# A new instruction order, new SBUF addresses and new PSUM banks for a hand-scheduled two-branch kernel

## The chip, the cores and the metric

The kernel runs on one core of a Trainium2 chip. The metric is device time in microseconds, as the median of the runs of one program. Five instruction streams work side by side and meet only through semaphores: PE (TensorE; its weight loads are listed apart as PEld), DVE (VectorE), ACT (ScalarE), POOL (GpSimd) and SP (SyncE, which here only issues DMAs). Each takes its own instructions strictly in the order in which they were written.

## What is computed

Two independent branches share one launch, and their outputs are concatenated. Branch A is a linear attention with softmax feature maps. Branch B is a state-space convolution: a kernel `K` of 2048 taps per channel is built from 256 complex modes, and the signal is convolved with it.

```python
def _A_ref(x, wqkv, w_phi, wo):            # x [1,2048,448], 16 heads of 28
    q, k, v = ...                           # x @ wqkv
    pq = einsum("bhsd,hdf->bhsf", q, w_phi); pk = ...
    phi_q = concat([softmax(pq), softmax(-pq)]); phi_k = ...
    kv = einsum("bhsf,bhsd->bhfd", phi_k, v); z = einsum("bhsf->bhf", phi_k)
    num = einsum("bhqf,bhfd->bhqd", phi_q, kv)
    den = einsum("bhqf,bhf->bhq", phi_q, z) + 1e-6
    return (num / den) @ wo
def _B_ref(u, A, B, C, log_dt, Dskip):     # u [1,2048,448], 256 modes
    P = exp(dt * A * l)                     # l = 0..2047
    K = einsum("dn,dnl,dn->dl", C, P, dt * B).real
    y = irfft(rfft(pad(u)) * rfft(pad(K)))[:2048]
    return y + u * Dskip
out = concat([a, b], axis=-1)
```

## The kernel before

Every step of the kernel is first recorded as a unit of a `Plan` (1399 units): what it costs on which engines, what it reads and writes, and a function that emits it. Nothing is scheduled while the kernel is built. Three tables of numbers at the top of the file decide everything that the program's text leaves open:

- `ORDER` lists all 1399 units in the order in which they are emitted, each with the letter of its engine: P for PE, D for DVE, A for ACT, G for POOL, S for SP. It sets the order within each engine's stream, and the engine itself where a unit may run on more than one.
- `HOMES` gives the byte address in SBUF of every buffer. Two buffers that share bytes make the later writer wait for the earlier reader.
- `BANKS` gives the PSUM bank of every accumulator. A matmul into a bank waits until the former tile there has been read.

```python
for x, bank in zip(self.tiles, BANKS):
    x.make(int(bank))
for token in ORDER.split():
    u = self.units[int(token[:-1])]
    u["fn"](names[token[-1]])
```

The units that the rest of the text speaks of, with the helper line under which the profile lists them:

- `mms` (L359): a group of matmuls into one PSUM tile. All PE work is listed there.
- `copy` (L350): a PSUM tile into SBUF, on ACT or on DVE as the order says. `act` (L340) is an activation on ACT; Exp and Sin need a table load between them (ACT_TABLE_LOAD). `tt` (L330) is elementwise work on DVE.
- `total` (L389 on DVE, L391 on POOL): an addition in SBUF, either by DVE or by a DMA from POOL's queue that adds.
- `dma` (L374): a transfer issued by SP, ACT or POOL. `turn` (L380): a transposing DMA, always from SP.

Branch B works in eight column groups `k`. For each, `dampings`, `rotations` and `hi_tables` make factors, `damp` combines them on DVE, and `build_k` multiplies them on PE: two units of 112 matmuls each, one into rows of 32 partitions and 49 columns, so that a unit has 224 instructions and is short. Two column groups make one channel group `gi` (0 to 3). Its taps go through `scatter_k`: four DMAs into a buffer `Kb`, then thirteen DMAs that place rows of `Kb` in `Kt` (the K rows), and one that fills `KX`. `kernel_spectrum` multiplies `Kt` with a transform table (units ks), `conv_group` multiplies the spectra on DVE (units conv), and `inverse` transforms back on PE, copies to `OB` and stores by SP. The spectrum of the signal, made early, is parked in DRAM (`SUd`) for groups 1 to 3 and read back.

Branch A works in 16 key tiles and then in four query blocks of four tiles. Each query tile ends with two copies of its numerators, a product, a `total`, a `turn` into `onT`, four matmuls with `wo`, a copy and a store by SP. The query tiles have no successors, and the order spreads them over the second half of the program.

Of the kernel before, what the change touches and what calls it, by code (L numbers as in the profile page):

```python
# [93 lines left out]
0A 29G 3S 1A 147S 4S 5S 2S 6S 59P 149S 7S 57D 50G 28S 40G 30G 9S 60A 46G 61D 8S 37G 52G 62P 41G 150S 48G 53G 217S 63P  # L94
25S 68A 33G 47G 65A 39G 69D 42G 86P 151S 31G 44G 70A 152S 35G 58D 36G 146S 84P 49G 87A 71D 54S 66A 88P 27S 85A 148S
93D 64A 89P 67A 15S 90D 232P 91D 218P 14S 220P 55G 222P 219D 79A 45G 156S 92D 226P 38G 72A 43G 22S 223D 81A 94D 82A
56G 95D 75A 51G 11S 722P 73A 83D 76A 23S 96P 727A 74D 730A 21S 725A 233A 77D 98A 728A 10S 726A 221D 165P 78A 109D 228P
100A 26S 729A 110D 719P 724A 17S 723A 102D 721A 163P 229D 227D 720A 167P 121D 12S 166A 224P 709P 168A 101D 225A 315P
99A 164A 112D 97A 171P 111D 161P 20S 159P 172D 169P 103D 711A 230P 16S 80D 157P 160A 231A 257P 162D 158A 104D 119A
170D 145S 105D 190P 19S 710A 712P 319D 191A 258D 196P 117A 106D 173P 114D 13S 179P 118A 108D 245P 174A 18S 120D 717A  # L100
214P 197A 716A 113D 193P 215A 240P 107D 124A 216S 115D 24S 181P 116D 234P 748D 194A 731G 198S 180A 251P 182A 732D 718A
291P 183S 733D 241A 125D 123A 205P 734G 252A 129P 752D 294G 295A 253S 782D 143P 130A 780S 131P 750D 206A 781D 238P
122A 132D 184P 783G 751D 126D 135P 235A 144A 735D 236P 136A 239A 137P 736D 266P 185A 246A 202P 713A 749D 737G 177P
237A 785D 714A 747G 139P 715A 141P 784D 138A 211P 140A 127A 199P 753D 786G 133P 242P 178A 134A 363P 243A 128A 254P
739D 200A 302P 914S 738D 267A 192S 272P 212A 247S 142A 195S 740D 290P 273A 186S 203A 201S 314P 292A 741D 268S 305A
742D 278P 274A 293A 743D 326P 304A 296S 745D 338P 329A 744D 316A 761P 317A 244S 746D 328A 259S 916D 756P 280A 213S
915D 207S 281A 788D 204S 763A 917G 255A 340A 787D 367A 754P 757A 789D 764A 762A 964D 341A 791D 767A 790D 256A 758P
765A 792D 755D 208P 759A 320S 918D 297P 766A 768P 760A 963S 965D 344S 771P 966D 209A 919D 175P 332S 187P 298D 794D
774A 155S 263P 793D 770A 799D 327P 769A 176D 795G 967D 279P 775A 920G 331A 275P 800D 772A 282G 968D 330G 269P 777A
797D 264A 260P 969G 773A 339P 261D 34G 270A 796G 798D 776A 333P 188A 398P 779A 189S 802D 343A 386P 276A 350P 283A 153S  # L110
778A 284S 374P 321P 801D 362P 271S 388A 299D 805P 400A 970D 401A 377A 404S 353A 921D 352A 356S 922D 803P 806A 262A
971D 308S 376A 389A 923D 364A 365A 472D 322D 895P 804A 972D 808S 285P 898A 248P 334D 901A 286D 896A 287D 351P 837S
392S 925D 899A 462G 345P 974D 892P 900A 924D 809S 897A 405P 893A 926D 357P 346D 309P 894A 928D 303P 32G 380S 358D 318G
930G 905P 323D 307A 306G 475D 310D 810S 289P 406D 393P 355D 301P 447P 394D 906A 311D 154S 387P 249D 909A 807S 451D
908A 902P 210S 913A 391D 288P 904A 300P 927D 313P 378G 325P 390G 312P 911A 929D 402G 381P 354G 836S 912A 450G 324P
335D 277S 410P 903A 827S 382D 933D 368S 337P 907A 815G 435P 931D 822G 910A 434P 935D 834S 818G 824S 932D 422P 438G
819S 812G 399P 934D 436A 813S 811G 936D 437A 446P 426G 823A 440S 817G 458P 403A 342G 366G 413A 336P 375P 439A 412A
369P 265A 973D 416S 937P 379A 975D 425A 825D 816A 370D 821S 347D 449A 407D 414G 448A 820G 383D 460A 939P 452S 977D
424A 250A 976D 938A 814S 359D 461A 371D 1084D 944P 940A 979G 1083S 1085D 428S 978D 349P 947A 441P 945A 348P 395D 417P
844S 360P 442D 948A 372P 464S 418D 411P 443D 946A 1086D 941P 950A 415D 949A 361P 943A 1087D 384P 843S 396P 408P 842S  # L120
373P 942A 954P 845S 1088D 429P 419D 453P 385P 430D 826S 951P 1089D 835S 955A 829S 397P 420P 953A 454D 851S 423P 455D
850S 952A 482P 1091D 884S 961A 409P 828S 421P 1133D 427A 465P 865S 956A 980D 459P 957A 838P 466D 852S 463A 431D 853S
962A 476P 982D 959A 984D 958A 433P 467D 432P 960A 830P 983D 839A 981D 445P 831A 846P 985D 840P 444P 832P 477A 854P
847A 479P 855A 483A 858D 457P 478A 456P 848P 841A 859D 468P 833A 856P 480A 986P 874D 857A 861G 849A 873D 875D 485P
876D 877G 988P 487A 481A 860D 486A 878D 987A 484A 470D 1064P 989A 1134D 1132S 471D 1090D 524P 1068A 1135G 504P 469P
540P 525A 473D 1092G 1069A 864D 496P 542A 885D 534P 880G 541A 866D 494P 1065A 862D 537P 497D 1066A 474D 1070A 495D
516P 526P 535A 517D 488P 708A 1137D 505A 514P 1067A 543P 863D 536A 489D 539A 1061P 515A 1136D 545A 506P 867P 990S
1062A 1093D 991S 1138G 507D 544A 1063A 527D 993G 554P 879D 1071P 538A 1099G 490D 1094D 1074P 992G 868D 546P 1095D
1072A 882D 572P 883D 870P 547D 1075A 1073A 1096D 881D 1076A 889P 1139D 1080A 573A 1097D 1082A 548D 564P 491D 1078A
1098G 1140D 598P 565A 890A 582P 1100D 584P 1077A 1141G 886P 1081A 1079A 1102D 1104D 583A 994G 1007S 1103D 871A 1101D  # L130
574P 585A 1000G 872S 562P 592P 887A 1002G 1003S 555A 549D 1105D 575A 552P 997G 891S 601P 553A 1001G 996S 563A 1113P
998G 1110P 1010S 1142D 594A 869S 1108P 593A 1143D 1009S 1111A 550D 1004S 1144G 492D 995S 603A 551D 1253D 1006G 599A
999S 493D 1114A 1106P 1005G 498D 602A 508D 600A 528D 509G 1119A 576D 1115A 586D 1116A 595P 1254D 1148G 1252S 1112A
518D 1117A 1123P 1255D 519G 1145D 596A 499D 597A 1146D 500S 1118A 1120P 566D 1147G 1257D 1019P 1034S 529G 604P 1124A
1256D 510S 1126A 1020D 1121A 1258G 1302D 1015P 1122A 1149D 587G 1125A 1023P 1016D 1127A 1151D 1017P 1150D 1130A 1011P
530S 1131A 1128A 1152D 1153D 1129A 1012A 1154D 1230P 1107A 1109A 1013P 1024A 1233P 1018A 1021P 1025P 1022A 588S 1014A
1260D 1155P 1026A 1259D 520S 1044D 1235A 1261G 1231A 1157P 1042D 1156A 1234A 1043D 1239A 1028D 1236A 1158A 1301G 1303D
1237A 1243P 1027D 577G 1232A 1268G 1262D 1238A 1240P 1046G 1263D 1029D 656P 1030G 1264D 650P 1247A 605D 1304G 1241A
653P 1266D 1248A 1265D 1246A 1244A 1045D 1242A 1271D 1269D 1245A 1161G 501P 606D 1249A 1272D 659P 1267G 1270D 1251A
1250A 511P 1160G 1273D 531P 1159G 1274D 521P 652A 1162G 532A 522A 512A 1282P 502A 1035D 658A 1277P 1053S 660A 1306D  # L140
1391S 661A 1283A 556D 1222S 1305D 654A 651A 1275P 1032D 1169G 1163S 1278A 1307D 1285A 1047G 1171S 657A 1033D 1284A
503S 1309D 1288A 1164S 655A 523S 1308D 1279P 1317G 1286A 1170S 1174G 662P 1287A 1031D 1173S 1172G 1280A 1310D 1292P
1168S 1165G 1281A 533S 1289P 1276D 1167G 1312D 1039P 1175G 1311D 1166G 663D 513S 1295A 567G 1178S 1293A 1313D 1036P
557G 1320D 1290A 664D 1314D 1291A 1315D 589P 1318D 1296A 1316G 1180P 1294A 1321D 1176G 1298A 1184P 1319D 1049G 1297A
1300A 1192P 1037A 1323D 1185A 1188P 558S 1193A 1299A 668P 700P 1181A 1186P 1203S 1189A 1182P 669A 1190P 1038S 1322D
1183A 670P 688P 578S 1187A 1196D 1324P 689A 1048D 1179S 1008D 1372S 1197D 568S 1050D 1326P 1325A 1054D 607D 665D 1052D
671D 1199D 666D 640P 1327A 1212D 559P 590A 1328S 1330G 1191A 698P 1051D 630P 1040A 1194P 1198D 1329G 641A 569P 667D
631A 1211D 1195A 680P 1331G 579P 681A 1202D 570A 1214D 620P 612P 580A 610P 1058P 611A 672D 613A 1216G 701A 608D 621A
1200D 560A 1204D 622P 690P 699A 642P 609D 632P 678P 614D 633A 1055P 623A 702D 691A 1201D 1335G 1334S 1333A 615D 1213D
1340G 1336S 1339A 1205P 1337G 1332S 624D 1338A 1343G 1342S 703D 643A 1215D 625G 1344S 1208P 1347S 634D 1345G 704S 644D  # L150
1341G 692D 1353P 1348S 1218D 616S 1357P 1177D 635D 1217D 1349P 1358A 673D 636S 1220D 679A 1219D 1354A 1361P 645D 1350A
# [93 lines left out]
class Bytes:  # L245
# [819 lines left out]
```

## Time and profile before

| | |
|---|---|
| median of 3 runs | 289.69 us (288.11 to 290.12) |
| the profiled execution, whole | 288.96 us |
| its span, first to last instruction | 287.2 us |
| time of it outside the span | 1.76 us |
| instructions in the span | 10986 |
| moved by DMA | 44.03 MB |
| mean granted TensorE clock | 0.974 of full speed |

Durations are those of the profiled execution. A page's busy time counts overlapping instructions of one engine once. "Idle before" an instruction is put down to the event that released it; "issue" means that the profile shows nothing that the engine waited for.

### The profile page before, as it was taken

To read this page: it belongs to the slowest core of one execution; us is meant where nothing else is said; L and a number is where in the kernel's file an instruction comes from. 1 tells how busy PE (TensorE), PEld (TensorE's weight loads), DVE (VectorE), ACT (ScalarE), POOL (GpSimd) and SP (SyncE) were. 2 spreads that over 40 slices of the span, in tenths; PEclk is the share of its full clock that TensorE was granted. 3 is DMA by queue.
4 is the path that set the end of the run, shared out by engine and by line. 5 is a ranking of instruction groups with operands and counts; after the bars stand their busy time and mean duration, and the time that the engine had idled before them with its cause. 6 is when DMAs were issued, how large, how long until landed. Compare 5 with 4: busy or idle time off the path is not lost.

```text
span 287.2 us, 10986 instructions
## 1 busy us (share of the span) xinstructions
PE 247.0 (86%) x4712; PEld 206.3 (72%) x4712; DVE 252.3 (88%) x373; ACT 232.7 (81%) x404; POOL 77.4 (27%) x132
## 2 busy tenths in 40 slices
PE   3674899899999899999999897988797997989890
PEld 2632488878977775888878787877467995889580
DVE  1569999999999999999999897999999698899960
ACT  3896999999999899699689987999988974708320
POOL 5830002211040105100143164503633902361000
PEclk9998999999999999999999999799989999999996
DMA  5979954766598979976179788796998777859864
GB/s 143 234 174 221 256 109 125 189 155 162 93 170 175 130 137 157 140 197 194 33 161 236 94 140 204 135 135 134 151 100 153 170 149 128 101 107 187 161 159 129
DMA packets 87273, 44.03 MB, mean 153 GB/s; under 512 B 68887, under 2 KB 84012, under 8 KB 86968
## 3 DMA queue, kind: packets, MB, share of 16 engines
q1 hardware_dynamic: 79010, 29.49, 49.8%
q0 software_dynamic: 6912, 12.12, 26.3%
q10 hardware_dynamic: 1302, 1.71, 1.8%
q8 instruction: 37, 0.61, 0.9%
q14 instruction: 12, 0.10, 0.1%
HBM read 13.72 MB, written 6.42 MB: 70 GB/s over the span
## 4 chain that ended last, share of the span: by engine, by line
PE 27%; DMA 10%; ACT 7%; issue 5%; DVE 4%; SPq 3%; POOL 2%; POOLq 0%; DVEq 0%; ACTq 0%
PE psum L359 27%; DMA sbuf<-sbuf 10%; ACT sbuf L340 4%; DVE sbuf L330 3%; ACT sbuf L350 2%; SPq L374 1%; SPq L380 1%; POOL sbuf L391 1%; POOL sbuf L374 1%; DVE sbuf L389 0%; ACT L340 0%; DVE sbuf L797 0%; POOLq L374 0%; ACTq L350 0%; DVEq L330 0%
## 5 line engine op out<-in xcount | busy, mean ns | idle before, releaser
L359 PE MATMUL psum<-sbuf 128*128 128x112 bf16 (+7 forms) x4712 | 247.0, 248 | 32.9 <-DMA sbuf<-in_B_u_dram 5.6
L359 PEld LDWEIGHTS <-sbuf 128*128 128x128 bf16 (+4 forms) x4712 | 206.3, 117 | 73.4 <-issue 31.0
L330 DVE TENSOR_TENSOR sbuf<-sbuf 128x896 bf16<-128x896 bf16 (+7 forms) x256 | 194.8, 812 | 11.8 <-PE psum L359 3.2
L340 ACT ACTIVATE sbuf<-psum 128x448 bf16<-128x448 f32 (+4 forms) x221 | 135.2, 710 | 9.1 <-PE psum L359 8.6
L350 ACT CAST sbuf<-psum 128x448 bf16<-128x448 f32 (+2 forms) x155 | 76.0, 568 | 32.9 <-PE psum L359 26.1
L391 POOL DMA_DIRECT2D sbuf<-sbuf x37 | 33.7, 1002 | 91.2 <-DVE sbuf L330 37.0
L374 POOL DMA_DIRECT2D sbuf<-sbuf x40 | 28.7, 777 | 62.5 <-DVE sbuf L330 31.2
L389 DVE TENSOR_TENSOR sbuf<-sbuf 128x896 bf16<-128x896 bf16 (+2 forms) x35 | 24.5, 706 | 0.3
L350 DVE CAST sbuf<-psum 128x448 bf16<-128x448 f32 (+1 forms) x33 | 19.7, 611 | 4.3 <-PE psum L359 3.5
L340 ACT ACT_TABLE_LOAD x16 | 20.5, 1283 | 2.0 <-PEq L1049 1.7
L330 DVE TENSOR_TENSOR sbuf<-psum,sbuf 128x896 f32<-128x896 f32 (+4 forms) x14 | 9.1, 659 | 6.2 <-ACT sbuf L340 3.9
L471 POOL TENSOR_SCALAR sbuf<-sbuf 128x128 bf16<-128x128 bf16 x16 | 8.5, 529 | 3.4 <-DMA sbuf<-const 2.3
L785 POOL MEMSET sbuf<- 128x16 bf16 x16 | 2.6, 222 | 20.8 <-DVE sbuf L330 16.5
L797 DVE RECIPROCAL sbuf<-psum 128x32 bf16<-128x32 f32 x16 | 5.2, 339 | 0.3 <-PE psum L359 0.2
L345 ACT CAST sbuf<-sbuf 128x1792 bf16<-128x1792 f32 x3 | 5.3, 1777 | 0.0
L731 POOL MEMSET sbuf<- 128x224 bf16 x8 | 3.3, 409 | 6.0 <-PE psum L359 6.0
L345 ACT CAST sbuf<-psum 128x896 bf16<-128x896 f32 x2 | 1.8, 909 | 2.9 <-PE psum L359 2.9
L839 DVE RECIPROCAL sbuf<-psum 128x128 f32<-128x128 f32 x4 | 3.8, 953 | 0.3 <-PE psum L359 0.3
L334 DVE SCALAR_TENSOR_TENSOR sbuf<-sbuf 128x64 f32<-128x64 f32 (+2 forms) x7 | 4.0, 586 | 0.0
L340 ACT ACTIVATE sbuf<-sbuf 128x1792 f32<-128x1792 f32 x2 | 3.5, 1736 | 0.0
L599 ACT ACTIVATE sbuf<-sbuf 128x896 bf16<-128x896 f32 x3 | 3.1, 1037 | 0.0
L478 DVE TENSOR_SCALAR sbuf<-sbuf 128x128 bf16<-128x128 bf16 x1 | 0.2, 194 | 3.2 <-DMA sbuf<-const 3.2
(15 smaller groups left out, 10.6 us busy)
## 6 DMA issues: line engine op xcount, KB each, us to landing
sbuf<-sbuf POOLq DMA_DIRECT2D x13, 448.0 KB, 5.2
sbuf<-sbuf POOLq DMA_DIRECT2D x18, 224.0 KB, 4.0
out_dram<-sbuf SPq DMA_DIRECT2D x32, 112.0 KB
sbuf<-SUd SPq DMA_DIRECT2D x6, 448.0 KB
sbuf<-const SPq DMA_DIRECT2D x16, 160.0 KB
SUd<-sbuf SPq DMA_DIRECT2D x19, 112.0 KB
sbuf<-in_B_u_dram SPq DMA_DIRECT2D x2, 896.0 KB
sbuf<-in_B_u_dram SPq DMA_DIRECT2D x8, 224.0 KB
```

Of the source, the lines that this page charges most:

```text
L330: lambda e: nc.vector.tensor_tensor(out=at(out_), in0=at(a), in1=at(b), op=op), [whose(a), whose(b)], [out_])
L334: lambda e: nc.vector.scalar_tensor_tensor(out=at(out_), in0=at(a), scalar=sc, in1=at(b), op0=op0, op1=op1),
L340: lambda e: nc.scalar.activation(at(out_), at(a), func, scale=scale, bias=bias), [whose(a)], [out_],
L345: plan.add({"ACT": 0.039 + sbuf + count(out_) * 0.8333e-3}, lambda e: nc.scalar.copy(at(out_), at(a)), [whose(a)], [out_])
L350: lambda e: (nc.scalar.copy if e == "ACT" else nc.vector.tensor_copy)(at(out_), at(a)), [whose(a)], [out_])
L359: nc.tensor.matmul(out_, lhsT=lhsT, rhs=rhs, start=start, stop=stop, **kw)
L374: plan.add({e: own[e] for e in engs}, lambda e: QUEUES[e].dma_start(out=out_, in_=in_, **kw), r, w, load=pieces / 16000 * max(28 + 0.025 * ...
L389: nc.vector.tensor_tensor(out=dst, in0=dst, in1=t2, op=ALU.add)
L391: nc.gpsimd.dma_start(out=view(dst), in_=view(t2), accum_op=ALU.add, max_dma_last_dim=3584)
L471: pool(0.25, lambda e, m=m: nc.gpsimd.tensor_scalar_mul(PID[:, m - 1, :], ident[:, :], float(m)), [ident[:, :]], [PID[:, m - 1, :]])
L797: nc.vector.reciprocal(rk[:, :, :].rearrange("p s h -> p (s h)"), zk.t[:, :])
L839: plan.add({"DVE": 0.868}, lambda e: nc.vector.reciprocal(rz[:, :, :, :], at(ndv(1))), [pz], [rz[:, :, :, :]])
```

## The change

No unit is added or removed, and the arithmetic is the same. `ORDER`, `HOMES` and `BANKS` are replaced as a whole; a line of each table stands here for the rest.

```diff
 ORDER = """
-0A 29G 3S 1A 147S 4S 5S 2S 6S 59P 149S 7S 57D 50G 28S 40G 30G 9S 60A 46G 61D 8S 37G 52G 62P 41G 150S 48G 53G 217S 63P
...
+33G 0S 36G 1S 29G 4S 149S 148S 6S 5S 59P 7S 57D 52G 146S 41G 51G 49G 60A 3A 47G 151S 61D 44G 2A 39G 62P 9S 40G 34G 48G
...
-HOMES = {"PID": [16000], "H": [36480], "AT": [7936], "TH": [184192], "PW128": [187776], "PW256": [178560], "PW512":
...
+HOMES = {"PID": [17024], "H": [29312], "AT": [7936], "TH": [184192], "PW128": [174976], "PW256": [165760], "PW512":
...
-0026446527374324761756040652675545444552051457146033221634377375467260731612465574363200622424205473\
...
+0026440304705621454650555754667221771130430106061647567571225642157020644635277572467504023236703331\
...
```

Units change engine as follows: of the PSUM copies, 29 go from DVE to ACT and 23 from ACT to DVE; of the totals, 12 go from DVE to POOL and 8 from POOL to DVE. Of the DMA issues, 14 come to ACT and 11 leave it, and 18 go each way between SP and POOL. ACT's stream has 15 table loads in place of 16.

The two builds of a column group stood one right behind the other for seven of the eight groups. Now three groups are so (0, 4 and 6), and in the other five something stands between. On PE, at the seam between the two builds of column group 7, the rows of before are these (32x49 is a matmul of a build; the wait is the first of the second build, for a PSUM bank that ACT frees):

```order
L359 LDWEIGHTS sbuf
L359 MATMUL psum<-sbuf 32x49
L359 LDWEIGHTS sbuf
L359 MATMUL psum<-sbuf 32x49 [waits Activation_49]
L359 LDWEIGHTS sbuf
```

At the end of the first of the two builds, the changed program has these rows (128x112 is a matmul of kernel_spectrum for channel group 2, which waits for the DMAs of its K rows, DMASW and DMAHW, and for a bank):

```order
L359 MATMUL psum<-sbuf 32x49
L359 LDWEIGHTS sbuf
L359 MATMUL psum<-sbuf 32x49
L359 LDWEIGHTS sbuf [waits DMASW5_49,DMAHW3_49,DMASW4_49,DMASW0_49]
L359 MATMUL psum<-sbuf 128x112 [waits Activation_49]
```

Fifty matmuls of kernel_spectrum and of the query numerators have moved in between the two builds of this group, and with them a wait for DMAs.

On SP, in the last part of the program, the rows of before from the K rows of channel group 3 (`64x1x112` and the like) on begin so; `SUd_59` is the parked spectrum of that group, and the DMA_TRANSPOSE rows are the turns of the query tiles:

```order
L374 DMA sbuf<-sbuf 64x1x112 x3
L374 DMA sbuf<-sbuf 24x1x112
L374 DMA sbuf<-sbuf 56x1x112
L374 DMA sbuf<-SUd_59 128x1792
L380 DMA_TRANSPOSE sbuf<-sbuf 128x4x128
L374 DMA sbuf<-SUd_59 128x1792
L380 DMA_TRANSPOSE sbuf<-sbuf 128x4x128 x3
L374 DMA out_dram<-sbuf 512x1x112
```

The changed program has this there:

```order
L374 DMA sbuf<-sbuf 64x1x112
L374 DMA sbuf<-sbuf 40x1x112
L374 DMA sbuf<-sbuf 56x1x112
L374 DMA out_dram<-sbuf 128x448
L380 DMA_TRANSPOSE sbuf<-sbuf 128x4x128 x4
L374 DMA sbuf<-sbuf 4x1x112
L374 DMA out_dram<-sbuf 512x1x112
L380 DMA_TRANSPOSE sbuf<-sbuf 128x4x128 x2
```

Two of SP's five K rows, and both loads of the parked spectrum, no longer stand behind the point at which `Kb` lands: from the first K row to the last store, SP issues 34 DMAs in place of 39.

On DVE, the last rows of before are these; 128x448 of L330 are the two subtractions that end the last product (the input of the last inverse), CAST rows are PSUM copies, L389 are totals:

```order
L389 TENSOR_TENSOR sbuf<-sbuf 128x1792 x2
L330 TENSOR_TENSOR sbuf<-sbuf 128x896
L389 TENSOR_TENSOR sbuf<-sbuf 128x896
L330 TENSOR_TENSOR sbuf<-sbuf 128x896
L350 CAST sbuf<-psum 128x448 x2
L330 TENSOR_TENSOR sbuf<-sbuf 128x448
L350 CAST sbuf<-psum 128x448
L330 TENSOR_TENSOR sbuf<-sbuf 128x448
L350 CAST sbuf<-psum 128x448
```

The changed program ends so:

```order
L389 TENSOR_TENSOR sbuf<-sbuf 128x1792
L389 TENSOR_TENSOR sbuf<-sbuf 128x896
L350 CAST sbuf<-psum 128x448
L330 TENSOR_TENSOR sbuf<-sbuf 128x896
L350 CAST sbuf<-psum 128x448
L330 TENSOR_TENSOR sbuf<-sbuf 128x896
L350 CAST sbuf<-psum 128x448 x2
L330 TENSOR_TENSOR sbuf<-sbuf 128x448 x2
```

Four copies stand ahead of the second subtraction where three stood, and the last copy has left DVE for ACT.

More of the change, by code (lines that the diff above doesn't have):

```diff
@@ L99 @@
[L99 to L113, printed above, removed]
@@ L200 @@
+235523406010066066026313672251020613462431351437152671644024066433333611223301"
 class Plan:
```

122 lines of the change are left out of this document (68 added, 54 removed), and 60 rows, old and new, of the table HOMES.

## The prediction

> **What bounds the kernel now.** I read the page's busy times first, then the same by stage, then the waits, the timeline of PE and last the end of the chain of waits.
>
> ```profile
> PE 247.0 (86%) x4712; PEld 206.3 (72%) x4712; DVE 252.3 (88%) x373; ACT 232.7 (81%) x404; POOL 77.4 (27%) x132
> ```
>
> The windows below (span of the window, then PE, PEld, DVE, ACT and POOL busy with counts, granted clock, DMA share, GB/s) cut the span where DVE first fills up and where the last build's copy ends.
>
> ```profile
> 0.00:28.72 28.72, 15.48 (x119) 10.91 (x120) 17.06 (x20) 21.14 (x30) 12.99 (x29) 0.96 0.85 193
> 28.72:241.70 212.98, 196.29 (x4027) 165.25 (x4025) 202.03 (x295) 192.30 (x333) 55.10 (x91) 0.98 0.79 152
> 241.70:287.20 45.50, 35.21 (x571) 30.16 (x569) 33.20 (x60) 19.30 (x43) 9.30 (x12) 0.95 0.74 135
> ```
>
> No single engine is the bound. In the middle 213 us DVE is busy 95%, PE 92%, ACT 90%, and each of them loses 11 to 21 us. What they lose it to:
>
> ```profile
> ACT sbuf L350 <- PE psum L359: 26.1, 22, 4.8
> ...
> ACT sbuf L340 <- PE psum L359: 8.6, 9, 2.4
> ...
> DVE sbuf L330 <- ACT sbuf L340: 7.0, 8, 3.9
> ...
> PE psum L359 <- DMA sbuf<-in_B_u_dram: 5.6, 2, 3.4
> DVE sbuf L330 <- PE psum L359: 5.5, 4, 2.3
> PE psum L359 <- ACT sbuf L340: 4.8, 6, 2.1
> ...
> PE psum L359 <- issue: 4.2, 5, 1.5
> ```
>
> ACT waits for PE (34.7 us), DVE for ACT and PE, PE for ACT and for "issue", that is for nothing that another engine does. The last is the sharpest row. Three of its five places are these on PE's timeline (start, length, what, count, idle before):
>
> ```profile
> 171.93 5.48 PE L359 MATMUL psum<-sbuf 128*32 128x49 bf16 x216 [0.25 <-DMA sbuf<-sbuf]
> 178.88 3.21 PE L359 MATMUL psum<-sbuf 128*32 128x49 bf16 x28 [1.48 <-issue]
> 218.12 3.84 PE L359 MATMUL psum<-sbuf 128*32 128x49 bf16 x128 [1.39 <-issue]
> 238.82 3.41 PE L359 MATMUL psum<-sbuf 128*32 128x49 bf16 x95 [0.93 <-issue]
> ```
>
> In the chain that ended last they stand as pieces of their own:
>
> ```profile
> 177.41 1.48 issue
> ...
> 216.73 1.39 issue
> ...
> 237.89 0.93 issue
> ```
>
> All three stop PE inside the second build of a column group, 3.80 us in sum. How far apart are they in instructions? The weight loads between their restarts, and the queue that brings instructions:
>
> ```profile
> 178.87:218.11 39.24, 26.56 (x636) 0.91 0.83 133
> 218.11:238.81 20.70, 18.68 (x510) 1.00 0.79 143
> ```
> ```profile
> q8 instruction: 37, 0.61, 0.9%
> ```
>
> A load and its matmul are two instructions: 1272 and 1020, with a few semaphore instructions 5 x 256 and 4 x 256. The queue brought 37 blocks of 0.61 MB / 37 = 16 KB. So PE runs out of instructions exactly where a block of 256 ends: the next block has not arrived. Builds use blocks up fastest: 216 matmuls in 5.48 us are 25 ns each, so 128 of them (a block) last 3.25 us.
>
> **The change, part by part.** *Instruction loading.* By the order, with boundaries every 256 PE instructions from the restarts above, and each unit at its own duration in this trace, seven blocks of before hold under 3.7 us of PE work (3.2 to 3.5; all lie in back-to-back pairs and hold at least 118 build matmuls of 128). Three of the seven stalled, 3.80 us in all, 0.54 per block. In the changed order four blocks are under 3.7 us (3.4 to 3.7): the pairs of column groups 1, 2, 3, 5 and 7 are parted, those of 0, 4 and 6 not. 4 x 0.54 = 2.2, so the term is **-1.6 us**. Bounds: -3.8 if none of the four stalls, +1.8 if all four do at the largest stall (4 x 1.4 = 5.6). The stalls at 178.88 and 218.12 belong to pairs that stay together, so I do not take the lower end.
>
> The Trainium skill ("Runtime: NRT & Kernel Launch", section "Instruction fetch mechanics") says that the sequencer fetches the next 16 KiB block of 256 instructions while it executes the current one, and that crossing a boundary costs little and is mostly hidden. The block size agrees with the 37 packets here; "mostly hidden" does not hold for the three boundaries inside builds. By it this term would be 0.
>
> *The end of SP's queue.* The chain's last pieces, and SP's own timeline:
>
> ```profile
> 268.31 3.55 DMA sbuf<-sbuf
> ...
> 271.90 7.96 PE psum L359 x124
> ...
> 279.89 0.53 ACT sbuf L350
> ```
> ```profile
> 251.45 3.61 SPq L374 DMA_DIRECT2D sbuf<-sbuf  x5
> ...
> 257.86 3.81 SPq L380 DMA_TRANSPOSE sbuf<-sbuf  x3
> ...
> 268.31 1.19 SPq L380 DMA_TRANSPOSE sbuf<-sbuf  x1
> ...
> 272.77 11.53 SPq L374 DMA_DIRECT2D out_dram<-sbuf  x17
> ```
>
> From 251.45 to 284.30 SP issues without a pause. The last copy ends at 280.42; seventeen stores at 0.68 us (11.53 / 17) put the last issue, which begins one store before 284.30, at 283.6, so that it waits 3.2 us in SP's queue. Of the 39 issues after the first K row five have gone elsewhere (two K rows, two reads of the parked spectrum, one early store): 5 x 0.7 = 3.5 us of SP's time, at the place where nothing but SP is late. What comes next is the last copy itself, with one store perhaps still ahead of it: 3.2 - 0.6 = **-2.6 us**. Bounds: -3.2, and 0 if SP meets one wait in its stretch; behind such a wait stand all later stores and, for 20 of them, nobody else waits. The K rows moved off SP go to POOL and ACT: five each, three on SP. A long row and a short one of issues on ACT's queue are
>
> ```profile
> 63.98 0.33 ACTq L374 DMA_DIRECT2D SUd<-sbuf  x1
> ```
> ```profile
> 251.48 2.70 ACTq L374 DMA_DIRECT2D sbuf<-sbuf  x3
> ```
>
> so five K rows there last 4.5 us at 0.9 each, against SP's 3.61 in before; they end at the same time as before within 1 us, and kernel_spectrum starts no later by them.
>
> *Work moved between DVE and ACT.* The rows by shape:
>
> ```profile
> L350 DVE CAST sbuf<-psum 128x448 bf16<-128x448 f32 x31 | 18.6, 617 | 3.8 <-PE psum L359 3.5
> ...
> L389 DVE TENSOR_TENSOR sbuf<-sbuf 128x1792 bf16<-128x1792 bf16 x11 | 11.7, 1074 | 0.1
> L389 DVE TENSOR_TENSOR sbuf<-sbuf 128x896 bf16<-128x896 bf16 x16 | 9.9, 616 | 0.2
> ...
> L389 DVE TENSOR_TENSOR sbuf<-sbuf 128x448 bf16<-128x448 bf16 x8 | 3.0, 378 | 0.0
> ```
> ```profile
> L350 ACT CAST sbuf<-psum 128x448 bf16<-128x448 f32 x135 | 67.4, 578 | 22.6 <-PE psum L359 16.5 <-DMA sbuf<-sbuf 3.1 <-issue 2.8
> L340 ACT ACT_TABLE_LOAD x16 | 20.5, 1283 | 2.0 <-PEq L1049 1.7
> ```
>
> DVE has 6 copies fewer (6 x 0.617 = 3.7), one total of 1792 more, two of 896 and three of 448 fewer (1.07 - 1.23 - 1.13 = -1.3): **5.0 us less**. ACT has 6 copies more (3.5), one table load less (1.28) and three DMA issues more; an issue takes 0.33 to 0.9 by the two rows above, 0.62 between them, so about 1.9: **4.1 us more**. PE has the same work. If each engine kept its idle time, the end would move by -5.0 (DVE), +4.1 (ACT), 0 (PE). ACT has the most idle time of the three in the waits above, 34.7 us of it behind PE, and takes the 4.1 largely there; DVE is the fullest. I take **-0.5 us**, near the mean of the three, and keep both ends.
>
> *The last product on DVE.* One more copy stands ahead of the second subtraction, on the path to the last inverse, at the 617 ns above: **+0.6 us**. The copy that left DVE's end was behind everything that is waited for; it is worth nothing.
>
> *At nothing.* The loads at the start are reordered on SP: both halves of `u` now come behind more transfers. PE waited 5.6 us for `u` in before; what covers a later arrival is ACT, which first makes the Sin and Exp tables in both orders (21.14 of 28.72 us busy) and only then copies the products of `u`. Without that cover a few us of the 5.6 would be added again. `HOMES` and `BANKS` make new waits and take old ones away; PE's waits for ACT (the 4.8 us row and its like) bound this from both sides. POOL is idle 210 us of the span, and four more totals at its queue (12 come, 8 go) have room.
>
> **Sum.** -1.6 - 2.6 - 0.5 + 0.6 = -4.1 us on the profiled execution of 288.96 us. That one is 0.7 us under the median of the three runs, so the forecast is 289.69 - 4.1 = **285.6 us**, 1.4% faster.
>
> **Rivals.** A measurement of this kernel can tell about 1% from no change, 286.8 to 292.6 us.
>
> *DVE sets the pace:* with its idle time unchanged its 5.0 us come through whole: 289.69 - 5.0 - 1.6 - 2.6 + 0.6 = 281.1. For it: 95% busy in the middle. Against it: it waits for ACT, which has more to do.
>
> *Loading was never the limit:* behind each stall PE would have waited for ACT or DVE, and the term is 0: 287.2. For it: two stalls lie in pairs that are unchanged. Against it: the stalls stand in the chain. The skill's page named above would give this time too.
>
> *New waits eat the gains:* the addresses and banks cost what the rest brings, 289.7. For it: a PE wait that goes is often followed by the next one.
>
> *ACT sets the pace, slower:* its 4.1 us are not absorbed. Its stream is in order; where a K row's issue waits for `Kb`, copies stand behind it, their banks stay full and PE stops. ACT's two rows of before that wait for PE turn round. It decides from the point where PE's waits for ACT grow by more than the 4.1 gained. The last copy is ACT's, so the gain at SP's queue is lost too: 289.69 + 4.1 - 0.8 (half the loading term) + 0.6 = 293.6. For it: 90% busy in the middle, and the last inverse now hangs on two copies of ACT. Against it: the idle time behind PE.
>
> **Chances.** Forecast, 283 to 288: 0.38. DVE, 280 to 283: 0.14. No loading limit, 286.5 to 288: 0.08. Gains eaten, 288 to 291.5: 0.12. ACT, 292 to 296: 0.28. Faster by over 1% is DVE's 0.14, three quarters of the forecast (0.29) and a little of the third, 0.46; slower is ACT's 0.28; the rest, 0.26, is within 1%. Range 280.5 to 295: it leaves out the end of DVE's case and of ACT's, about 0.15. The likeliest case alone has 283 to 288.
>
> **What would show it.** PE's "issue" row falls from 4.2 us to about 2.5, with no stall in column groups 1, 2, 3, 5, 7. SP's last store begins within 0.7 us of the last copy's end. DVE is busy about 247 us, ACT about 235. Wrong would be: PE's waits for ACT above 11 us, ACT's busy share at nine tenths where PE has gaps, or stalls on "issue" outside the builds.

## The result and the profile after

The changed kernel takes 287.88 us as the median of 20 runs (283.63 to 291.50), the kernel before 289.12 us in 20 runs of the same comparison (286.63 to 291.49): a ratio of 0.9897 with a 95% interval of 0.9861 to 0.9932, about 3 us. The ratio leaves out runs over 1.5% above the fastest of their kernel; that takes ten of the changed kernel's twenty and two of the other's, and over all forty the means differ by 0.5% (289.06 and 287.66 us). Six more runs of the changed kernel beside the old one, given below as an experiment, came to 0.9856 (0.9798 to 0.9914). So it is faster by about 1%, perhaps by half of that, near the edge of what can be told from no change. The forecast was 285.6 us, the range 280.5 to 295.0.

The profiled execution of the changed kernel is the longest of its twenty: 291.50 us, a span of 289.7 us. Its page, busy times first, then the waits (engine and tile, releaser: sum in us, count, longest):

```profile
PE 248.9 (86%) x4712; PEld 208.1 (72%) x4712; DVE 247.8 (86%) x363; ACT 234.2 (81%) x409; POOL 79.4 (27%) x134
```
```profile
ACT sbuf L350 <- PE psum L359: 35.4, 25, 3.5
DVE sbuf L330 <- DMA sbuf<-sbuf: 8.1, 5, 4.2
DVE sbuf L330 <- ACT sbuf L340: 6.8, 4, 6.0
...
PE psum L359 <- issue: 5.0, 6, 1.9
PE psum L359 <- DVE sbuf L330: 4.8, 3, 4.0
...
PE psum L359 <- ACT sbuf L340: 4.4, 3, 3.7
PE psum L359 <- ACT sbuf L350: 4.2, 10, 1.0
...
PE psum L359 <- DMA sbuf<-const: 2.2, 1, 2.2
```

DVE and ACT are as busy as the order said. But PE's row "issue", which was to fall from 4.2 to about 2.5 us, stands at 5.0. On PE's timeline (start, length, what, count, idle before) the stalls have left their old places and come up at new ones, the first of them not in a build at all:

```profile
170.17 0.91 PE L359 MATMUL psum<-sbuf 112*128 112x112 bf16 x15 [0.55 <-issue]
...
176.56 4.07 PE L359 MATMUL psum<-sbuf 128*32 128x49 bf16 x128 [1.32 <-issue]
...
207.49 2.26 PE L359 MATMUL psum<-sbuf 128*32 128x49 bf16 x55 [0.88 <-issue]
...
249.63 10.66 PE L359 MATMUL psum<-sbuf 128*128 128x112 bf16 x179 [1.89 <-issue]
...
261.68 21.88 PE L359 MATMUL psum<-sbuf 128*128 128x112 bf16 x355 [0.46 <-DMA sbuf<-sbuf]
```

The end, on SP's and on ACT's timeline:

```profile
270.05 1.25 SPq L380 DMA_TRANSPOSE sbuf<-sbuf  x1
271.39 15.47 SPq L374 DMA_DIRECT2D out_dram<-sbuf  x20
```
```profile
283.60 0.53 ACT L350 CAST sbuf<-psum 128x448 bf16<-128x448 f32 x1 [1.34 <-PE psum L359]
```

SP still runs twenty stores in one go, and its last one begins at 286.3 (286.86 less one store), 2.2 us behind the last copy at 284.13. Before, the last store began at 283.77, 3.4 us behind the last copy. The end lies 5.6 us behind that copy, 6.8 us before.

Where did the lead come from? The table takes from the trace of each profiled execution when PE has done a given share of its work (each group of matmuls weighted by the shortest time that it took in any of the profiles). The last rows are experiments that are described below.

| kernel, its profiled execution | 5% | 20% | 40% | 60% | 80% | 100% | span |
|---|---|---|---|---|---|---|---|
| before | 28.8 | 67.7 | 119.3 | 165.5 | 228.0 | 279.9 | 287.2 |
| changed | 25.8 | 66.6 | 116.8 | 166.9 | 231.5 | 283.6 | 289.7 |
| changed, again | 25.2 | 66.0 | 116.4 | 164.5 | 225.9 | 277.0 | 283.2 |
| changed, six stores on POOL | 25.0 | 65.9 | 116.3 | 166.8 | 229.1 | 280.3 | 285.3 |
| before, u loaded earlier | 28.5 | 67.7 | 119.1 | 165.4 | 227.5 | 279.6 | 287.4 |
| before, seven stores on POOL | 28.2 | 67.1 | 119.1 | 165.4 | 225.8 | 282.5 | 286.7 |
| changed, u loaded later | 28.1 | 68.5 | 118.8 | 167.3 | 231.5 | 282.7 | 288.4 |
| changed, u loaded earlier | 26.9 | 68.1 | 118.4 | 168.9 | 232.0 | 284.4 | 290.3 |

The three executions of the changed order with `u` where the change puts it lead the kernel before by 3.0 to 3.8 us in the first twentieth and by 2.5 to 3.0 us at 40%. By 60% the lead is 1.0 us in the best and gone in the two others. From there the spread between executions of one order (6.6 us at the end) is larger than what the orders differ by: at 80% the best execution of either order stands at 225.8 or 225.9 us.

### The profile page after: what moved, and what is told of

It is laid out like the page before. It is cut to its first block, busy times and chain, and to the rows that moved or that the text cites. A ratio compares the mean times of both kernels' runs of the same rounds, so it can differ in the third digit from the quotient of the medians.

```text
span 289.7 us, 11014 instructions
## 1 busy us (share of the span) xinstructions
PE 248.9 (86%) x4712; PEld 208.1 (72%) x4712; DVE 247.8 (86%) x363; ACT 234.2 (81%) x409; POOL 79.4 (27%) x134
## 3 DMA queue, kind: packets, MB, share of 16 engines
q0 software_dynamic: 7456, 12.78, 28.2%
## 4 chain that ended last, share of the span: by engine, by line
PE 37%; ACT 18%; DMA 15%; DVE 13%; issue 8%; POOL 3%; SPq 3%; ACTq 0%; DVEq 0%; POOLq 0%
PE psum L359 37%; DMA sbuf<-sbuf 12%; DVE sbuf L330 10%; ACT sbuf L340 9%; ACT sbuf L350 6%; SPq L374 3%; POOL sbuf L374 3%; ACT L340 1%; DMA sbuf<-in_B_B_re_dram 1%; DMA sbuf<-const 1%; ACT sbuf L345 1%; ACT sbuf L599 1%; DVE sbuf L389 1%; POOL sbuf L391 1%; DVE sbuf L350 1%
## 5 line engine op out<-in xcount | busy, mean ns | idle before, releaser
L330 DVE TENSOR_TENSOR sbuf<-sbuf 128x896 bf16<-128x896 bf16 (+7 forms) x256 | 194.7, 809 | 18.7 <-DMA sbuf<-sbuf 8.1
L340 ACT ACTIVATE sbuf<-psum 128x448 bf16<-128x448 f32 (+3 forms) x221 | 135.6, 727 | 7.4 <-PE psum L359 5.5
L350 ACT CAST sbuf<-psum 128x448 bf16<-128x448 f32 (+3 forms) x161 | 79.7, 577 | 41.4 <-PE psum L359 35.4
L391 POOL DMA_DIRECT2D sbuf<-sbuf x41 | 37.9, 1004 | 112.7 <-DVE sbuf L330 57.7
L374 POOL DMA_DIRECT2D sbuf<-sbuf x40 | 28.3, 750 | 25.7 <-DVE sbuf L797 13.9
L389 DVE TENSOR_TENSOR sbuf<-sbuf 128x896 bf16<-128x896 bf16 (+2 forms) x31 | 23.2, 759 | 0.3
L350 DVE CAST sbuf<-psum 128x448 bf16<-128x448 f32 (+2 forms) x27 | 15.9, 592 | 3.4 <-PE psum L359 3.4
L330 DVE TENSOR_TENSOR sbuf<-psum,sbuf 128x896 f32<-128x896 f32 (+4 forms) x14 | 9.1, 661 | 8.1 <-ACT sbuf L340 6.0
L468 POOL MEMSET sbuf<- 64x448 bf16 x3 | 1.4, 466 | 17.1 <-DVE sbuf L330 17.0
L785 POOL MEMSET sbuf<- 128x16 bf16 x16 | 3.3, 224 | 2.6 <-DVE sbuf L330 2.6
```

The lines of the kernel that those rows point to most:

```text
L330: lambda e: nc.vector.tensor_tensor(out=at(out_), in0=at(a), in1=at(b), op=op), [whose(a), whose(b)], [out_])
L340: lambda e: nc.scalar.activation(at(out_), at(a), func, scale=scale, bias=bias), [whose(a)], [out_],
L350: lambda e: (nc.scalar.copy if e == "ACT" else nc.vector.tensor_copy)(at(out_), at(a)), [whose(a)], [out_])
L374: plan.add({e: own[e] for e in engs}, lambda e: QUEUES[e].dma_start(out=out_, in_=in_, **kw), r, w, load=pieces / 16000 * max(28 + 0.025 * ...
L389: nc.vector.tensor_tensor(out=dst, in0=dst, in1=t2, op=ALU.add)
L391: nc.gpsimd.dma_start(out=view(dst), in_=view(t2), accum_op=ALU.add, max_dma_last_dim=3584)
```

## Experiments

Orders are given as units in the sequence in which they are emitted, with the engine's letter; what is not shown is unchanged.

**What makes a stall: `m_load`.** TensorE alone, with nothing beside it and with four kinds of traffic.

```python
def builds(n):                        # 768 per stretch, 32 columns of weights, 49 of data
    ...
longs(ps[1], 40); nc.scalar.copy(ld[0][:, :, 0], ps[1][:, 0:8]); load(0); builds(768)
longs(ps[2], 40); nc.scalar.copy(tot[0][:, :, 0], ps[2][:, 0:6]); totals(0); builds(768)
```

> This kernel leaves the whole computation out: it stores zeros and then runs TensorE alone through five stretches of 768 matmuls shaped like those of a build (32 columns of weights, 49 of data), about 25 ns each, so that a block of 256 instructions holds some 3.2 us of work. Ahead of each stretch stand 40 long matmuls (512 columns). Beside the stretches run: 1 nothing; 2 eight loads of 448 KB on SP; 3 six accumulating transfers of 448 KB on POOL; 4 eight transfers in pieces of 56 bytes on SP; 5 the loads of 2 and the totals of 3 together. Theory 'block length alone' (the rule of the prediction's loading term): the same stalls in all five stretches, 0.5 to 1.4 us at every boundary or at none. Rival 'traffic': in stretch 1 no gap above 0.3 us, the refill of 16 KB starts within 0.7 us of the boundary and has landed 2 us behind it; in stretches 2, 3 and 5 it starts 1 us or more late and TensorE stands 0.5 to 3 us at each boundary; TensorE goes on 1.3 to 1.8 us after the refill has landed in all of them.

PE's timeline in the first stretch (nothing beside it) and in the third (totals on POOL):

```profile
57.13 1.52 PE L61 MATMUL ps<-W,U 128*32 128x49 bf16 x128 [2.46 <-issue]
61.13 1.52 PE L61 MATMUL ps<-W,U 128*32 128x49 bf16 x128 [2.48 <-issue]
64.59 1.52 PE L61 MATMUL ps<-W,U 128*32 128x49 bf16 x128 [1.93 <-issue]
...
123.77 1.52 PE L61 MATMUL ps<-W,U 128*32 128x49 bf16 x128 [6.09 <-issue]
131.06 1.53 PE L61 MATMUL ps<-W,U 128*32 128x49 bf16 x128 [5.77 <-issue]
```

Every stall is followed by exactly 128 matmuls, 256 instructions, but for the last of a stretch, where the long matmuls take over. The matmuls took 12 ns and not the 25 expected, so that PE stood at every boundary in every stretch, and "no gap in stretch 1" was wrong. But that shows the supply itself: 3.46 to 4.00 us from restart to restart with nothing else moving. The trace has every refill of the instruction queue as one packet of 16 KB. From the records of that queue, in us behind the restart named first:

```
restart   refill starts   lands   next restart   beside it
 61.13        +1.05       +2.12      +3.46       nothing
 82.74        +3.50       +4.61      +5.92       loads on SP
116.48        +4.83       +5.76      +7.29       totals on POOL
153.97        +2.47       +3.43      +4.83       56-byte pieces on SP
184.97        +5.66       +6.54      +8.12       loads and totals
```

The transfer takes about 1 us each time and PE goes on 1.2 to 1.6 us after it has landed. What traffic lengthens is the wait before the refill starts, from 1.1 to 1.6 us in the quiet stretch to as much as 5.7 us. "Block length alone" falls.

**Real builds: `m_pairs`.** The same with the accumulating, strided matmuls of the kernel, in stretches of two, four and eight builds, then with loads and with totals.

> This kernel leaves the whole computation out and stores zeros. TensorE runs builds (112 matmuls each, accumulated and with the strided operands of the real ones, so that a block of 256 instructions should hold about 3.2 us of work) back to back, first with nothing beside them: three times two, twice four, once eight builds, parted by 36 long matmuls; then two, two, four and four builds with four loads of 448 KB on SP, and the same with three accumulating transfers of 448 KB on POOL, each begun ten long matmuls ahead of the builds. Rule of the prediction (every block under 3.7 us costs 0.54 us): about 0.5 us per block, the same in all three parts. Theory 'supply' (from the first stand-alone kernel: a refill takes 3.5 to 4.0 us from boundary to boundary when nothing else moves, and longer under traffic): without traffic at most 0.3 us at the first boundary of a stretch, then 0.3 to 0.8 us at each further one; with loads 1 to 3 us and with totals 2 to 5 us at the first boundary.

Nothing beside it (two builds, four, eight), then four builds with loads, then four with totals:

```profile
44.09 5.63 PE L61 MATMUL ps<-W,U 128*32 128x49 bf16 x224
...
84.35 11.18 PE L61 MATMUL ps<-W,U 128*32 128x49 bf16 x448
...
122.17 12.86 PE L61 MATMUL ps<-W,U 128*32 128x49 bf16 x521
135.48 3.27 PE L61 MATMUL ps<-W,U 128*32 128x49 bf16 x128 [0.45 <-issue]
...
203.28 3.26 PE L61 MATMUL ps<-W,U 128*32 128x49 bf16 x128 [3.06 <-issue]
...
276.90 3.28 PE L61 MATMUL ps<-W,U 128*32 128x49 bf16 x128 [2.87 <-issue]
```

A block is 3.26 us of work here. Without traffic a pair of builds never stalls, nor do four in a row, where "supply" had expected short stalls; the first stall comes after 521 matmuls. With loads the pairs stalled 1.9 and 2.0 us at one boundary. With totals the two pairs show no stall, since the block asked for behind the start of the totals was needed only in the long matmuls that follow (PE stood 0.65 us there once), and the fours stalled 2.9 and 3.3 us. So a pair of builds is harmless by itself, and a boundary close behind the start of a large transfer is not. The Trainium skill ("Runtime: NRT & Kernel Launch", section "Instruction fetch mechanics") says that the next block is fetched while the current one runs and that crossing is mostly hidden. The quiet pairs and fours of `m_pairs` agree; its stretches under traffic, and `m_load` even when quiet (1.9 to 2.5 us at each boundary), do not.

**The pairs parted, by themselves: `b_part`.**

```diff
 kernel before, PE
-1106P build4.0   595P qe2.1
+595P qe2.1   1106P build4.0
-1275P build6.0   1279P exps7.0
+1279P exps7.0   1275P build6.0
-1190P ks2.2.1   670P q3.0   ...   1324P build7.0   1326P build7.1
+...   1324P build7.0   1190P ks2.2.1   670P q3.0   1326P build7.1
```

> The kernel before with three back-to-back pairs of builds parted by TensorE work that stood next to them (groups 4 and 6 by one unit, group 7 by two), all else as it was. If the length of a block decides and a stall that goes comes through (the prediction's loading term): the stalls of 1.48, 1.39 and 0.93 us behind those pairs fall to under 0.5 us in sum, PE's row 'issue' from 4.2 to about 1 us, and the time falls by 2 to 4 us (ratio 0.987 to 0.993). If loading was never the limit: the row falls the same way, PE's waits for ACT, DVE or a DMA grow by as much, ratio 0.997 to 1.003. If it is the DMA traffic that decides: one or two of the three stay above 0.7 us.

The three stalls went, PE has no row "issue" left among its larger waits, and the kernel became slower: 293.44 us (291.58 to 294.43) against 288.98, ratio 1.0127 (1.0070 to 1.0184). None of the expectations had that. Its PE timeline around the second place, and the waits:

```profile
213.65 3.58 PE L359 MATMUL psum<-sbuf 128*128 128x112 bf16 x120 [0.20 <-ACT sbuf L350]
219.87 5.51 PE L359 MATMUL psum<-sbuf 128*128 128x112 bf16 x160 [2.64 <-ACT sbuf L340]
```
```profile
PE psum L359 <- ACT sbuf L340: 11.1, 11, 2.6
```

The unit that was pulled ahead, `exps7.0`, needs a bank that ACT empties only at 219.87. Behind the build that moment lay hidden under a stall and 3 us of work; ahead of it PE stands 2.64 us. PE's waits for ACT's activations went from 4.8 to 11.1 us, more than the stalls had cost.

**The same order of PE, other traffic: `b_dma`.**

```diff
 kernel before, SP
-1010S su1   1009S su1   ...   1252S hi6.0
+...   1252S hi6.0   1010S su1   1009S su1
-1391S ud3.1   1222S ud2.1            (behind 1053S ud1.1)
+1391S ud3.1   1222S ud2.1   1053S ud1.1
-1203S ud2.0   1179S su2   1372S ud3.0  (8 to 12 us behind 1178S su2)
+1178S su2   1179S su2   1203S ud2.0   1372S ud3.0
```

> The kernel before with TensorE's order unchanged, back-to-back pairs and all; seven loads of SP (two of the parked spectrum of group 1, one of group 2, four of u) that were in flight beside the three stalls are issued earlier or later. 'Block length alone': the three stalls stay at 0.9 to 1.5 us each, 3.8 us in sum. 'Traffic': their refills start within 1 us of the boundary (1.8 to 2.4 us before) and the three fall to under 1.5 us in sum, PE's 'issue' row from 4.2 to about 1.5; the time falls by up to 2 us (0.993 to 1.0) unless the moved loads come late for DVE.

It takes 295.51 us (293.08 to 298.88), 1.0195 (1.0123 to 1.0268). PE's order is that of before to the instruction, and its stalls are not:

```profile
179.42 2.27 PE L359 MATMUL psum<-sbuf 128*32 128x49 bf16 x28 [0.19 <-issue]
196.26 3.28 PE L359 MATMUL psum<-sbuf 128*32 128x49 bf16 x128 [1.39 <-issue]
203.01 1.59 PE L359 MATMUL psum<-sbuf 128*32 128x49 bf16 x56 [3.46 <-issue]
226.41 20.19 PE L359 MATMUL psum<-sbuf 128*32 128x49 bf16 x510 [2.60 <-issue]
248.25 15.52 PE L359 MATMUL psum<-sbuf 128*32 128x49 bf16 x303 [1.65 <-issue]
```
```profile
PE psum L359 <- issue: 9.8, 6, 3.5
...
DVE sbuf L330 <- DMA sbuf<-sbuf: 10.9, 6, 6.8
```

The first, where the loads were taken away, fell from 1.48 to 0.19 us. The two later ones were to fall and grew (1.39 to 2.60, 0.93 to 1.65), and two new ones, 1.39 and 3.46 us, stand in the builds of group 5: ahead of the longer one the refill started 4.2 us behind the boundary, 0.3 us at the same boundary of the kernel before. The sum went from 4.2 to 9.8 us, well beyond the 1.8 to 4.2 us that executions of the old traffic show, so the traffic decides. The median rose by 6.5 us. How much of that is the stalls is not shown: this profile is of the longest of the six runs, 9.8 us longer in span than that of the kernel before, and the moved loads also made DVE wait 10.9 us for DMAs instead of 1.9. Where a moved load will do harm I did not foresee.

**The end of SP's queue: `b_sptail`, `a_sptail`.**

```diff
 kernel before, last seventeen stores
-1060S 888S 1207S 591S 1210S 1229S 687S
+1060G 888G 1207G 591G 1210G 1229G 687G
 changed kernel, last twenty
-561S 707S 1226S 581S 1379S 687S
+561G 707G 1226G 581G 1379G 687G
```

> The kernel before with seven of the last seventeen stores issued on POOL's queue instead of SP's. If the prediction's term for the end of SP's queue is right: the last store is issued within 0.7 us of the last copy's end (3.2 us behind it before), time -2.0 to -2.6 us, ratio 0.991 to 0.993. If the transfers themselves, not their issues, end the kernel: the last store is issued earlier but the end moves by less than 0.8 us, ratio 0.997 to 1.003.

> The changed kernel with six of its last twenty stores issued on POOL's queue. SP's last store came 2.2 us behind the last copy's end. If SP's issues end the kernel: the last store within 0.8 us of the last copy, time -1.4 us against the changed kernel unaltered (ratio to before 0.985 to 0.992). If, as in the kernel before with seven stores moved, what SP gives at the end is lost to the transfers ahead of the last products: within 0.5 us of the changed kernel unaltered.

With seven stores away, SP's last store of `b_sptail` begins 0.3 us behind the last copy (3.4 before) and the end lies 3.7 us behind it (6.8). Yet the time is that of the kernel before: 288.72 us, 0.9993 (0.9950 to 1.0036). SP and PE ahead of the end:

```profile
267.18 1.19 SPq L380 DMA_TRANSPOSE sbuf<-sbuf  x1
...
272.01 11.89 SPq L374 DMA_DIRECT2D out_dram<-sbuf  x10
```
```profile
271.81 10.68 PE L359 MATMUL psum<-sbuf 128*128 128x448 bf16 x124 [3.38 <-DMA sbuf<-sbuf]
```
```profile
271.80:282.50 10.70, 10.68 (x124) 8.38 (x124) 3.54 (x7) 1.40 (x3) 0.56 (x1) 0.73 0.45 112
```

PE was 2.7 us ahead of the kernel before by 262 us in this execution (its three stalls were 0.62, 0.51 and 0.66 us long instead of 3.80 in sum), but the transposing load that its last products need is issued at 267.18, only 1.1 us earlier than before, because it stands in SP's queue behind other loads and stores. PE waits 3.38 us for it. On SP the stores that I moved stood behind that transfer; on POOL four of them were issued from 261.8 to 264.8 us, ahead of it. Beside them one store ahead of it took SP 1.77 us (0.57 before), and the load took 4.58 us (3.55 before). So the move may itself have cost part of what it saved, which no run here separates. In this execution the granted clock also fell to 0.73 in the last stretch (1.00 before), 2.7 us; whether it does so in the other eleven runs the times cannot tell. `a_sptail`: 287.37 us, 0.9889 (0.9845 to 0.9933), the end 4.4 us behind the last copy instead of 5.6; against 287.17 of the unaltered kernel on the same chip, 1.1 us cannot be told.

**The changed kernel again: `a_again`.** Unaltered.

> The changed kernel once more, unaltered, since its profiled execution was the longest of its twenty. Theory 'its stalls on instructions vary from execution to execution': the stalls stand at the same boundaries (170, 177, 207, 250 us, give or take 2) with other lengths, their sum 2 to 5 us (5.0 before), the execution 286 to 289 us, and what it is shorter by is within 1 us of what the stalls and the end behind the last copy are shorter by. Rival 'another wait made it long': the same stalls, and PE's waits for ACT, DVE and DMAs shorter by the difference. Against the kernel before: 0.990 to 0.997.

287.17 us (283.62 to 290.25) beside 290.10; the profiled execution is 285.06 us, with these stalls:

```profile
177.79 6.09 PE L359 MATMUL psum<-sbuf 128*128 128x112 bf16 x84 [0.64 <-issue]
223.31 4.07 PE L359 MATMUL psum<-sbuf 128*32 128x49 bf16 x127 [1.02 <-issue]
227.90 14.03 PE L359 MATMUL psum<-sbuf 128*128 128x112 bf16 x382 [0.52 <-issue]
242.16 10.66 PE L359 MATMUL psum<-sbuf 128*128 128x112 bf16 x179 [0.23 <-issue]
```
```profile
PE 244.4 (86%) x4712; PEld 204.0 (72%) x4712; DVE 247.5 (87%) x363; ACT 233.8 (83%) x409; POOL 79.6 (28%) x134
```

The sum is 2.4 us instead of 5.0, partly at other boundaries of the same order; "the same boundaries" was wrong, and so was the expectation that stalls and the end make up the difference within 1 us. PE is busy 4.5 us less for the same matmuls, at a mean granted clock of 0.990 instead of 0.970. Stalls and clock, 2.6 + 4.5, are a little more than the 6.5 us by which the spans differ; the end behind the last copy is 5.6 us in both. PE's other waits changed as well (for ACT's activations from 4.4 to 1.0 us, for DMAs between buffers from 1.2 to 4.3) and about cancel.

**The engines without their order: `b_homes`, `a_homes`.** Only the 72 copies and totals that the change moves to or from DVE change engine, for instance:

```diff
 kernel before with these units on the engines of after (b_homes)
-495D q0.0   1276D build6.0   1394D inv3.1   502A q0.0
+495A q0.0   1276A build6.0   1394A inv3.1   502D q0.0
```

> The kernel before with its own order, addresses, banks and DMA queues, and only the 72 copies and totals that the change moves to or from DVE on their engines of the changed kernel: the prediction's term for work moved between DVE and ACT by itself. DVE's busy time 252 to about 247.5 us, ACT's 233 to about 235.5. Prediction's term: -0.5 us (ratio 0.997 to 1.000). If DVE sets the pace: -4 to -5 us (0.983 to 0.987). If ACT does: +3 to +5 us (1.010 to 1.017). If order and homes hold only together, since the order is laid out for the moment at which each engine is free: more than +5 us (above 1.017), PE's waits for ACT and DVE grow.

> The changed kernel with the same 72 copies and totals back on the engines that they had before; order, addresses, banks and DMA queues are those of the changed kernel. DVE's busy time 247.8 to about 252.5 us. If the gain is that of the order (loading and SP's end): the ratio to the kernel before stays at 0.990 to 0.997. If DVE's lighter load is the gain: 1.000 to 1.005. If order and homes hold only together: above 1.01.

`b_homes` 325.62 us, 1.1245 (1.1194 to 1.1296); `a_homes` 323.47 us, 1.1187 (1.1127 to 1.1247). DVE's busy time moves as the term said, 252.3 to 247.5 in `b_homes` and 247.8 to 253.1 in `a_homes`, and says nothing about the time: either mixture is 12% slower. The waits of `b_homes`:

```profile
ACT sbuf L350 <- PE psum L359: 50.3, 26, 7.4
...
DVE sbuf L330 <- DMA sbuf<-sbuf: 24.3, 8, 7.8
PE psum L359 <- ACT sbuf L350: 17.8, 18, 4.6
```

Engines and order hold only together, so the term for moved work cannot be measured by itself.

**The head: `b_head`, `a_head`, `a_u`.** After the table above.

```diff
 kernel before, SP (b_head)
-217S ua1   25S inw0   ...   15S inx2   14S inx2   156S ua0
+217S ua1   156S ua0   25S inw0   ...   15S inx2   14S inx2
 changed kernel, SP (a_head)
-147S late   156S ua0   217S ua1   12S inx1   152S late   13S inx1
+147S late   217S ua1   12S inx1   152S late   13S inx1   156S ua0
 changed kernel, SP (a_u)
-8S inBre   11S inx0   28S inv   147S late   156S ua0   217S ua1
+8S inBre   156S ua0   11S inx0   217S ua1   28S inv   147S late
```

> The kernel before with one instruction moved: the load of the first half of u is issued on SP right behind that of the second half (at about 9 us instead of 20.0 us), nine loads earlier. If the changed kernel's lead of about 3 us at TensorE's first twentieth of work comes from that load, and if it comes through to the end: TensorE's second wait for u (3.4 us at 25.9) goes, the first (2.2 us at 16.0) grows by up to 1.5 us, and the time falls by 1.5 to 3.5 us (ratio 0.988 to 0.995). Rival 'the head is not on the path': the waits go the same way, ACT and DVE or later waits take their place, ratio 0.997 to 1.003. If the loads behind it now come late for the first copies: above 1.003.

> The changed kernel with the load of the first half of u issued later on SP, at about 18 us instead of 11.1 us (as in the kernel before, where it was 20.0 us). If the head carries the gain: TensorE waits for it 2 to 4 us at about 19 us, and the time rises by 1.5 to 4 us against the changed kernel unaltered, ratio to the kernel before 0.994 to 1.004. Rival 'the head is not on the path': within 1 us of the changed kernel unaltered, 0.985 to 0.991.

> The changed kernel with both halves of u a little earlier on SP: the first at about 8.4 us instead of 11.1 us, the second at about 10.4 us instead of 11.6 us. If TensorE's remaining wait for u (3.3 us at 17.9) is on the path: 1 to 2 us faster than the changed kernel unaltered (ratio to before 0.979 to 0.988). If ACT, which makes its tables until 19 us, sets the pace there: within 0.7 us of it.

`b_head`: 289.83 us, 1.0038 (1.0004 to 1.0072), no faster. The second wait for `u`, 3.39 us before, is gone, and PE stands nearly as long at the same place for DVE:

```profile
15.62 5.83 PE L359 MATMUL psum<-sbuf 128*128 128x448 bf16 x28 [2.11 <-DMA sbuf<-in_B_u_dram]
...
26.07 3.14 PE L359 MATMUL psum<-sbuf 128*128 128x448 bf16 x20 [2.58 <-DVE sbuf L350]
```

`a_head`, the undoing in part (the first half of `u` is issued at 15.9 us, not 11.1): 289.00 us, 0.9968 (0.9926 to 1.0010). PE waits 4.13 us for `u` and reaches a twentieth of its work at 28.1 us:

```profile
20.94 8.33 PE L359 MATMUL psum<-sbuf 128*128 128x448 bf16 x40 [4.13 <-DMA sbuf<-in_B_u_dram]
```

Against the unaltered kernel's 0.9897 and 0.9856 that is 0.7 to 1.1%, 2 to 3 us, about what the change brought; it overlaps the first of the two intervals at its edge. `a_u` did not help: 287.12 us, 0.9952 (0.9919 to 0.9985), its wait for `u` 3.9 us; that B's inputs and `u` then share the same transfers is a guess. So the early `u` makes the lead at the head, and in the old order it gains nothing by itself. That this lead is what comes through to the end is likely, not shown: the unaltered kernel was not run beside these two, their ratios are 0.2% apart though one loads `u` late and the other early (their medians 1.9 us), and in the table `a_head` is no later at 80% and at the end than the first profile of the unaltered kernel.

## Why the prediction came close, point by point

The forecast was 2.3 us under the median, which lies inside its range, but its sum is not how it came about: that it came close is luck. The experiments show one term wrong and one too large by half, and a lead of 3 us where the sum had nothing.

**Instruction loading, -1.6 us: wrong.** The step that failed: "seven blocks of before hold under 3.7 us ... Three of the seven stalled, 3.80 us in all, 0.54 per block". The row "issue" is 5.0, 3.8 and 2.4 us in three executions of the changed order and 4.2, 3.8 and 1.8 us in three with PE's old order (the kernel before, `b_head`, `b_sptail`): means of 3.7 and 3.3, no gain; `a_u` and `a_head`, also with PE's changed order, have 5.2 and 6.1. The quiet pairs of `m_pairs` never stall; the refill's start decides, and `b_dma` moved the stalls with PE's order untouched. Whether a stall that goes is gained, against the second rival, stays open: `b_part` lost its stalls and became slower, and `b_dma` changed other waits too. The sign named in advance, stalls outside the builds, is there at 170.17 and 249.63.

**The end of SP's queue, -2.6 us: half.** The end came 1.2 us closer to the last copy. The count of issues fell as forecast, but twenty stores (seventeen before) stand behind the last transposing load, so SP is 2.2 us late where 0.7 were allowed. `b_sptail` shows what the argument left out: SP also delays a load that PE waits for ahead of the last products, and moving seven stores to POOL gave nothing in time although the end came 3.1 us closer to the last copy.

**Work moved between DVE and ACT, -0.5 us: busy times right, price open.** DVE 247.8 us for about 247, ACT 234.2 for about 235, PE's waits for ACT 4.4 + 4.2 = 8.6 us, under the 11 that would have spoken for the slower rival. The rival's other sign did come: from 196.1 to 200.1 us PE stands and ACT is busy 3.99 of the 4.00 us. But DVE is busy 3.90 us there, and the profile puts that wait (3.98 us) to DVE. The step from busy times to time has no measurement: `b_homes` and `a_homes` show that the engines of the copies and totals can't be moved without their order.

**The last product on DVE, +0.6 us: not seen.** PE runs its last 21.88 us without a gap, so it does not wait for that subtraction.

**The head, "at nothing": the largest miss.** The text feared a later `u`, and it misread the order: "both halves of `u` now come behind more transfers" holds for one half only. The half that PE waited for longer went from the 23rd to the 16th place in SP's stream (issued at 20.0 us before, at 11.1 now); the other went from the 13th to the 17th (8.0 and 11.6 us). In the kernel before PE's second wait for it ends at 25.90 us; in the changed one both halves are there when the only wait ends, at 17.88 us in its second profile:

```profile
25.90 3.69 PE L359 MATMUL psum<-sbuf 128*128 128x448 bf16 x22 [3.39 <-DMA sbuf<-in_B_u_dram]
```
```profile
17.88 4.56 PE L359 MATMUL psum<-sbuf 128*128 128x448 bf16 x14 [3.27 <-DMA sbuf<-in_B_u_dram]
```

Seven copies of the products of `u` went from DVE to ACT with that, two the other way. PE is 3.0 us or more ahead at a twentieth of its work, and `a_head`, without most of that lead, is about as slow as the kernel before. The cover named there, ACT's tables, exists (in the first profile of the changed kernel it is ACT that PE waits for here, 3.67 us up to 18.33); it does not make up for the second wait, 3.4 us, that the old order lost.

**Where the lead goes again** was in no term. Thirteen loads of filters follow each other on SP from 124 us, and the first of `kernel_spectrum`'s units waits for one that is issued late among them, at 131.8 us:

```profile
124.35 9.32 SPq L374 DMA_DIRECT2D sbuf<-const  x13
```
```profile
135.68 31.65 PE L359 MATMUL psum<-sbuf 128*128 128x112 bf16 x676 [2.17 <-DMA sbuf<-const]
```

That is 1.7 to 2.3 us in all three executions of the changed order, and none or 0.5 us in the three with PE's old order and the old loads. Two of the three also had a granted clock of 0.86 between 130 and 142 us. Issuing the tiles that `ks0.0.0` needs ahead of the others would be the next thing to try; it was not tried, and no version run here is shown to beat the changed kernel.

## What to carry to other kernels

Count instruction boundaries together with the transfers that are in flight there: two or four builds in a row (25 ns a matmul) did not stall with nothing beside them, and did behind a large load or total. Read the first 30 us of a trace as carefully as its middle: one early load with the work arranged behind it made the only lead here, 3 us, that stands out from the spread of single executions. And when one wait is removed, look up what the next unit needs at that moment, above all its accumulator bank, before counting the wait as gained.

## What the runs showed of the hardware

A refill is one 16 KB packet that is asked for when PE passes a boundary and is needed at the next one. It took about 1 us to move and PE went on 1.2 to 1.8 us after it landed, in every stall that I followed, so that 3.5 to 4.0 us per 256 instructions is the best that PE got when it used them faster. In `m_load`, accumulating transfers from POOL and 448 KB loads from SP delayed its start to +3.5 to +5.7 us. I had not expected the same program to stall at different boundaries in different executions (2.4 to 5.0 us in sum), nor a granted clock that falls for some 10 us at a time at places that change (0.73 at the end of one execution, 0.86 at 130 us in two): between the two profiles of the changed kernel they come to 7.1 us where the spans differ by 6.5, and single runs of one unaltered kernel lie 5 to 9 us apart.
